# A hand-written order of 5341 pieces of work, replaced by another order of the same pieces

## The chip, the cores and the metric

The kernel runs on one core of a Trainium2 chip. The metric is device time in microseconds (us) of one execution. Before the change three runs gave 816.19, 816.78 and 819.2 us; their median is 816.78 us. A core has five engines, each of which works through its own list of instructions from the first to the last: TensorE (PE in the profile, with its weight loads as PEld), VectorE (DVE), ScalarE (ACT), GpSimd (POOL) and SyncE (SP, which here only issues transfers). They wait for each other through semaphores alone.

## The reference, cut to what matters

There are 8 batches of 8 heads with 576 positions and 64 features. First comes a thresholded attention per head, then a mixture of four causal attention experts over the 512 joined features of a batch, each position using the two experts with the largest gate:

```python
scores = scale * np.matmul(q, k.transpose(0, 1, 3, 2))
thresh = np.max(scores, axis=-1, keepdims=True) - tau
scores = np.where(scores >= thresh, scores, -1000000000.0)
attn = softmax(scores); x = np.matmul(attn, v)      # joined over heads: (B, S, 512)
for e in range(4):
    q, k, v = x @ wq[e], x @ wk[e], x @ wv[e]
    a = softmax(causal(scale * (q @ k.T)))
    out += (mask of the top 2) * gate weight * (a @ v @ wo[e])
```

## The kernel before, in words

Heads are taken in pairs: a pair fills the 128 partitions with 2 x 64 features. `n` counts the 32 pairs, four to a batch. For each pair the program has these pieces:

- `ldk`, `ldq`, `ldv`: transfers of keys, queries and values, issued by SP in its list's order (a few at the start by ACT).
- `tk`, `tq`: TensorE transposes keys and queries (line 1240). Then `kr`, `qr` copy them out of PSUM, `kh`, `qh` round them to the high part, and `kl`, `ql` subtract to get the low part (line 1087, in two halves). Products are made as high x high + high x low + low x high.
- `s`: scores, for five tiles of queries (numbered 4, 2, 3, 0, 1); tile 4 is the 64-position tails of both heads. It is the `kk,qq` matmuls of line 1103.
- `min` (line 1203, DVE): copies a score row block out of PSUM and finds its extremum. `exp` (line 1216, ACT). `thr`: a tiny sum. `stt` (line 1220, DVE): compares with the threshold, multiplies and sums. `eps1`, `rec1`: tiny. `pn` (lines 1498 and 1496): scales the rows, on POOL, ACT or DVE.
- `tm`: TensorE transposes the scaled rows (line 1240); `pt` copies them out (lines 1079, 1081, named `pa` and `pt`). `av`: the product with the values. `xr`, `xh`, `xl`, `xd` copy it out and split it into the high and low part of `x`.

After a batch's four pairs come its expert pieces: `pj` (projections, `x,wh` and `x,wl` matmuls), `v` (values and gates), `s2`, `s2t`, `nm`, `p2`, `p2s`, `t2`, `pt2`, `bv`, `zh`, `zl`, `o`, `ob`, `st`, alike in kind. The weights are loaded, rounded (`wh`) and subtracted (`wl`) once, during the first pairs; the first projection needs all of them and all of the first batch's `x`. Where a matmul group must cross the two halves of the array, a tiny fence instruction (`fs`, `fpj`, `fv`, `fo`, `fs2t`, lines 1357 and 1359) on another engine stands between its two parts.

What sets the order is a table written out by hand, `ORDER`: for each family of pieces one global place per piece, in 0 to 5340. `work()` makes the pieces, `plan()` goes through them by place and emits each on its engine, so that each engine's list is the sorted table cut down to that engine. A second table, `BY`, has for each piece that may run on several engines one digit, which of them it takes (0, 1 or 2 in the order in which the piece names its engines):

```python
x = Task({e: (u[0] - u[1], u[0]) for e, u in t.items()}, fn, deps, takes, uses, cols, ld, name, ORDER[family][i], by)
for t in sorted(tasks, key=lambda t: t.place):
```

`plan()` also picks the buffer slots and PSUM banks and puts a few small filler matmuls (`tri`) on TensorE at the start, from costs written in the file; these costs are the same before and after. The engines still wait on semaphores for real data, so a place in the tables decides what an engine waits for and never what is computed.

Of the kernel before, what the change touches and what calls it, by code (L numbers as in the profile page):

```python
# [248 lines left out]
def work(K):  # L249
# [320 lines left out]
    for n in range(NPR):  # L570
# [1019 lines left out]
```

## Time and profile before

| what | us |
|---|---|
| three runs | 816.19, 816.78, 819.2 |
| the profiled execution, its own time | 816.84 |
| its span from first to last instruction | 815.1 |
| TensorE busy | 791.2 |
| VectorE busy | 730.3 |
| ScalarE busy | 697.7 |
| GpSimd busy | 423.3 |

The profiled execution took 816.84 us, 0.06 us more than the median of the runs; 1.7 us of it lie around the span. An engine is busy while one of its instructions runs; waiting and issuing are not counted. A stretch's busy time is read from the view by windows, the wait in front of an instruction from the timeline, where it stands in square brackets with the engine that ended it.

### The profile page before, as it was taken

The numbers are of one execution on the slowest core, as the hardware profiler recorded it, in microseconds if no ns is written. First come the engines' busy times: TensorE is split into PE (matmuls) and PEld (weight loads), VectorE is DVE, ScalarE is ACT, GpSimd is POOL, SyncE is SP. The second block draws the span as 40 slices with busy tenths as digits, with TensorE's granted clock in tenths as the row PEclk, the third lists the DMA queues.
The fourth block names the chain that finished last, engine by engine and source line by source line (L and its number), as shares of the span: only waits on it lengthen the run. The fifth ranks groups of instructions, "written<-read, shape, count | busy, mean of one in ns | idle before, by whom it ended". The sixth has DMA issues, their size and how long they took to land.

```text
span 815.1 us, 34755 instructions
## 1 busy us (share of the span) xinstructions
PE 791.2 (97%) x14117; PEld 731.0 (90%) x14117; DVE 730.3 (90%) x2331; ACT 697.7 (86%) x1449; POOL 423.3 (52%) x811
## 2 busy tenths in 40 slices
PE   9888999999999999999999999999999999999998
PEld 7777898899988999888998999889998899988997
DVE  6999989998989989898989988998999988999584
ACT  5989888997899868998899988999999987999475
POOL 5998625753445345544365435455345563468232
PEclk9999999999999999999999999999999999999999
DMA  4433212112132112222222122202311212220002
GB/s 115 89 80 72 66 38 45 42 45 52 39 83 55 37 47 50 55 64 52 46 54 64 43 73 55 61 14 69 80 42 38 67 45 50 59 55 3 15 27 80
DMA packets 140240, 44.21 MB, mean 54 GB/s; under 512 B 135216, under 2 KB 135216, under 8 KB 140080
## 3 DMA queue, kind: packets, MB, share of 16 engines
q1 hardware_dynamic: 138512, 41.65, 20.9%
q8 instruction: 111, 1.82, 1.0%
q10 hardware_dynamic: 1568, 0.34, 0.2%
q14 instruction: 49, 0.40, 0.2%
HBM read 32.51 MB, written 9.44 MB: 51 GB/s over the span
## 4 chain that ended last, share of the span: by engine, by line
PE 76%; DVE 9%; ACT 6%; POOL 5%; issue 3%; DMA 1%; SPq 0%; DVEq 0%; ACTq 0%; POOLq 0%
PE ps L1103 64%; PE ps L1240 10%; DVE e L1203 3%; PE ps L1093 3%; POOL e L1498 2%; DVE e L1220 2%; ACT pt L1079 1%; ACT e L1216 1%; DMA ki<-in_k_dram 1%; ACT e L1475 1%; DVE e L1470 1%; POOL sm L1213 1%; ACT pa L1079 0%; DVE pt L1081 0%; ACT e L1490 0%
## 5 line engine op out<-in xcount | busy, mean ns | idle before, releaser
L1498 POOL TENSOR_SCALAR e<-e,sm 128x576 f32<-128x576 f32 (+4 forms) x277 | 193.5, 708 | 82.0 <-DVE sm L1231 55.3
L1203 DVE TENSOR_SCALAR_CACHE_REDUCE e<-ps 128x576 f32<-128x576 f32 x288 | 209.5, 752 | 21.2 <-PE ps L1103 15.5
L1216 ACT ACTIVATE e<-e,sm 128x576 f32<-128x576 f32 x288 | 215.3, 771 | 10.9 <-DVE e L1203 8.8
L1220 DVE SCALAR_TENSOR_TENSOR e<-e,sm,e 128x576 f32<-128x576 f32 x256 | 209.4, 841 | 2.4 <-ACT e L1216 0.7
L1103 PE MATMUL ps<-kk,qq 64*128 64x288 f32 x1900 | 176.1, 309 | 5.7 <-POOL kk L1087 1.3
L1103 PEld LDWEIGHTS ps<-kk,qq 64*128 64x128 f32 x1900 | 139.9, 186 | 16.1 <-DVE e L1203 3.4
L1079 ACT ACTIVATE pt<-ps 128x640 f32<-128x640 f32 (+3 forms) x228 | 142.5, 639 | 13.1 <-PE ps L1093 5.4
L1103 PE MATMUL ps<-pt,vm 128*64 128x128 f32 (+1 forms) x1536 | 143.9, 259 | 0.0
L1240 PE MATMUL ps<-ident,e 64*128 64x64 f32 x2624 | 123.8, 226 | 7.1 <-DVE e L1203 2.7
L1103 PEld LDWEIGHTS ps<-pt,vm 128*64 128x64 f32 x1536 | 127.3, 137 | 2.7 <-issue 0.7
L1240 PEld LDWEIGHTS ps<-ident,e 64*128 64x128 f32 x2624 | 108.8, 139 | 19.1 <-issue 5.1
L1103 PE MATMUL ps<-pa,vm 128*64 128x128 f32 x1024 | 124.4, 274 | 0.0
L1103 PEld LDWEIGHTS ps<-pa,vm 128*64 128x64 f32 x1024 | 110.7, 137 | 3.3 <-issue 1.2
L1103 PE MATMUL ps<-x,wh 64*128 64x288 f32 x1024 | 106.0, 296 | 0.0
L1213 POOL TENSOR_TENSOR sm<-sm 128x2 f32<-128x2 f32 (+1 forms) x127 | 41.9, 333 | 121.7 <-DVE e L1220 82.5
L1496 ACT ACTIVATE e<-e,sm 128x576 f32<-128x576 f32 (+4 forms) x116 | 83.2, 730 | 5.9 <-DVE sm L1231 4.8
L1103 PEld LDWEIGHTS ps<-x,wh 64*128 64x128 f32 x1024 | 84.2, 185 | 0.6 <-ACT kk L1142 0.2
L1103 PE MATMUL ps<-x,wl 64*128 64x288 f32 x512 | 78.5, 292 | 0.0
L1475 ACT ACTIVATE e<-e,sm 128x384 f32<-128x384 f32 (+3 forms) x128 | 70.9, 557 | 1.6 <-DVE sm L1470 1.0
L1079 ACT ACTIVATE pa<-ps 128x512 f32<-128x512 f32 x105 | 62.2, 595 | 7.0 <-PE ps L1240 6.8
L1470 DVE CUSTOM_DVE_ANT_0 e<-ps,tri 128x384 f32<-128x384 f32 (+3 forms) x128 | 58.4, 484 | 3.7 <-PE ps L1103 2.9
L1359 POOL TENSOR_SCALAR fencePOOL<-eps 128x2 f32<-128x2 f32 x56 | 16.7, 298 | 83.5 <-PE ps L1103 80.1
(153 smaller groups left out, 1656.5 us busy)
## 6 DMA issues: line engine op xcount, KB each, us to landing
vm<-in_v_dram SPq DMA_DIRECT2D x64, 128.0 KB, 2.6
out_dram<-ob SPq DMA_DIRECT2D x32, 256.0 KB, 2.4
ki<-in_k_dram SPq DMA_DIRECT2D x63, 80.0 KB, 2.5
qi<-in_q_dram SPq DMA_DIRECT2D x63, 80.0 KB, 2.5
ki<-in_k_dram SPq DMA_DIRECT2D x63, 64.0 KB, 2.4
vt<-in_v_dram SPq DMA_DIRECT2D x128, 16.0 KB, 2.2
qi<-in_q_dram SPq DMA_DIRECT2D x31, 64.0 KB, 2.4
qi<-in_q_dram SPq DMA_DIRECT2D x31, 48.0 KB, 2.4
```

The lines of the kernel that those rows point to most:

```text
L1079: self.nc.scalar.activation(dst, src, AF.Copy)
L1093: self.nc.tensor.transpose(self.ps[:, bank, c * n:(c + 1) * n], x[sl], self.ident[sl, sl])
L1103: return self.nc.tensor.matmul(out, x, y, start=first, stop=last)
L1203: self.nc.vector.tensor_scalar(self.sides(sc), self.dbank(s)[:, :, :HS], 0.0, None, op0=ALU.add, op1=ALU.min, accum_out=self.small(sm)[:, ...
L1213: self.nc.gpsimd.tensor_tensor(m[:, to:to + n], m[:, of:of + 2 * n:2], m[:, of + 1:of + 2 * n:2], op=ALU.add)
L1216: self.nc.scalar.activation(self.row(e), self.row(sc), AF.Exp, bias=self.small(sm)[:, 2 * j:2 * j + 1], scale=-1.0)
L1220: self.nc.vector.scalar_tensor_tensor(self.row(e), self.row(sc), m[:, 8 + j:9 + j], self.row(e), op0=ALU.is_le, op1=ALU.mult, accum_out=m[ ...
L1240: self.nc.tensor.transpose(self.ps[:, g.slot + h, c * D:(c + 1) * D], x, self.ident[sl, sl])
L1470: self.nc.vector.tensor_tensor_reduce(self.row(p2)[:, :w], self.dbank(g)[:, j, :w], self.tri[:, SM - w:], 1.0, FAR, op0=ALU.add, op1=ALU.m ...
L1475: self.nc.scalar.activation(p, p, AF.Exp, bias=m[:, 2 * j:2 * j + 1], scale=-1.0, accum_out=m[:, 4 + 2 * j:5 + 2 * j])
L1496: self.nc.scalar.activation(p, p, AF.Copy, scale=x)
L1498: (self.nc.vector if e == "DVE" else self.nc.gpsimd).tensor_scalar(p, p, x, 0.0, op0=ALU.mult, op1=ALU.add)
```

## The change

Only the numbers of the two tables change: nearly every place in `ORDER`, and many digits of `BY`. Two families of the second table show the kind of edit:

```diff
-    "xd": "00100011000100000000000000001111",
+    "xd": "00001000010000000100010000001011",
-    "kl": "000000010000000000000000000000000000",
+    "kl": "000000001000000000000000000000000000",
```

No piece is added or dropped. TensorE keeps the same 12140 instructions, the 89 filler matmuls among them, in a slightly different order. DVE goes from 1757 to 1738 instructions, ACT from 1313 to 1339, POOL from 816 to 809, SP stays at 599. Of the row scalings (lines 1498 and 1496), DVE had 39 and gets 15; ACT had 116 and gets 147; POOL had 277 and gets 270.

Two places show how the lists differ. The first is GpSimd's list where it prepares the keys of the fourth pair. `kk1_...` and `qq1_...` are that pair's keys and queries, `wh` and `wl` the weights' high and low part, `e` score rows, `x` and `iv` the first attention's output, `sm` small sums. Before:

```order
L1087 TENSOR_TENSOR kk1_61_918<-pt3_53_821,kk1_61_918 128x320
L1213 TENSOR_TENSOR sm_80<-sm_80 128x2
L1087 TENSOR_TENSOR qq1_63_936<-pt1_50_787,qq1_63_936 128x320
L1498 TENSOR_SCALAR e2_58_870<-e2_58_870,sm_80 128x576
L1087 TENSOR_TENSOR wl2_125<-ob0_54_823,wh2_122 128x256
L1083 TENSOR_SCALAR wh2_122<-sm_80 128x4
L1087 TENSOR_TENSOR wl2_125<-ob1_47_760,wh2_122 128x256
L1083 TENSOR_SCALAR x10_72_1030<-iv2_71_1026 128x256
L1087 TENSOR_TENSOR kk1_61_918<-pt3_53_821,kk1_61_918 128x320
```

And GpSimd's list at the same place with the change:

```order
L1498 TENSOR_SCALAR e7_45_730<-e7_45_730,sm_80 128x576
L1083 TENSOR_SCALAR qq1_60_922<-pt0_44_707 128x640
L1083 TENSOR_SCALAR x00_49_789<-iv1_46_742 128x256
L1083 TENSOR_SCALAR wh2_122<-ob2_28_505 128x256
L1083 TENSOR_SCALAR kk1_67_970<-pt3_56_858 128x640
L1087 TENSOR_TENSOR qq1_60_922<-pt0_44_707,qq1_60_922 128x320
L1087 TENSOR_TENSOR kk1_67_970<-pt3_56_858,kk1_67_970 128x320 x2
L1087 TENSOR_TENSOR qq1_60_922<-pt0_44_707,qq1_60_922 128x320
```

The second half of the keys' low part stood eight instructions behind the first, with two weight subtractions, a rounding of `x` and a row scaling between; now both halves follow each other.

The second place is VectorE's list just ahead of the first batch's first projection. `x20` and `x30` are the outputs of the third and fourth pair, `x00` and `x10` of the first and second. Before:

```order
L1087 TENSOR_TENSOR x20_109_1510<-iv4_95_1367,x20_109_1510 128x64
L1498 TENSOR_SCALAR e0_106_1500<-e0_106_1500,sm_80 128x576
L1220 SCALAR_TENSOR_TENSOR e5_111_1521,sm_80<-e4_104_1468,sm_80,e5_111_1521 128x576
L1203 TENSOR_SCALAR e1_117_1621,sm_80<-ps_63 128x576
L1203 TENSOR_SCALAR e2_118_1623,sm_80<-ps_63 128x576 x2
L1087 TENSOR_TENSOR x20_109_1510<-iv4_95_1367,x20_109_1510 128x320
L1087 TENSOR_TENSOR x00_46_758<-iv1_49_785,x00_46_758 128x256
L1220 SCALAR_TENSOR_TENSOR e5_111_1521,sm_80<-e4_104_1468,sm_80,e5_111_1521 128x576
L1074 TENSOR_REDUCE sm_80<-sm_80 128x2
L1231 RECIPROCAL sm_80<-sm_80 128x2
L1087 TENSOR_TENSOR x30_116_1619<-iv2_114_1592,x30_116_1619 128x320
```

And VectorE's list at the same place with the change, down to the last of the four `x` that the projection needs:

```order
L1203 TENSOR_SCALAR e3_116_1631,sm_80<-ps_63 128x576
L1203 TENSOR_SCALAR e0_118_1635,sm_80<-ps_63 128x576 x2
L1081 COPY pt1_122_1669<-ps_63 128x640
L1087 TENSOR_TENSOR wl1_124<-ob1_110_1527,wh1_121 128x256
L1087 TENSOR_TENSOR x30_120_1647<-iv0_115_1606,x30_120_1647 128x320
L1203 TENSOR_SCALAR e4_127_1738,sm_80<-ps_63 128x576
L1087 TENSOR_TENSOR x10_105_1464<-iv2_70_1027,x10_105_1464 128x320
L1087 TENSOR_TENSOR qq1_113_1590<-pt3_112_1580,qq1_113_1590 128x320
L1203 TENSOR_SCALAR e4_127_1738,sm_80<-ps_63 128x576
L1081 CAST x30_120_1647<-iv0_124_1731 128x256
L1087 TENSOR_TENSOR x30_120_1647<-iv0_124_1731,x30_120_1647 128x256
```

The row scaling and the subtractions for `x20` and `x00` have left VectorE's list (they run on other engines), and a weight subtraction, a copy out of PSUM and a rounding of `x30` have come to it. Counted from the start to the last of these subtractions, VectorE had 141 pieces of the table and now has 132; GpSimd, down to its own last piece that the projection needs, had 102 and now has 106.

## Rows read from the trace of the kernel before

**Rows 1.** Stretches: length, busy us (instructions) of PE, PEld, DVE, ACT, POOL, then PE's clock:

```profile
0.00:91.00 91.00, 79.53 (x1231) 67.85 (x1233) 81.19 (x228) 73.89 (x131) 76.08 (x127) 0.98 0.38 87
91.00:100.00 9.00, 9.00 (x150) 9.00 (x149) 8.98 (x26) 7.84 (x15) 3.01 (x6) 1.00 0.27 60
100.00:700.00 600.00, 592.65 (x10774) 552.15 (x10773) 553.11 (x1775) 531.37 (x1104) 291.42 (x572) 1.00 0.22 52
700.00:815.10 115.10, 110.07 (x1974) 101.96 (x1970) 87.01 (x306) 84.58 (x202) 52.82 (x109) 1.00 0.13 38
```

**Rows 2.** The same view of 20 to 91 us alone:

```profile
20.00:91.00 71.00, 61.34 (x1068) 53.56 (x1067) 67.92 (x187) 62.80 (x115) 65.84 (x92) 0.98 0.35 78
```

**Rows 3.** PE's waits, 0 to 91 us: who waited for whom, us, times, longest:

```profile
PE ps L1240 <- POOL e L1498: 2.5, 5, 0.8
PE ps L1103 <- DVE eps L983: 1.5, 1, 1.5
PE ps L1103 <- POOL kk L1087: 1.3, 1, 1.3
```

**Rows 4.** PE's waits from 91 us to the end, the longest total and the last:

```profile
PE ps L1103 <- ACT pt L1079: 1.4, 4, 0.5
...
PE ps L1240 <- ACT pt L1079: 0.2, 1, 0.2
```

**Rows 5.** Timeline of POOL: start us, us, instruction, [idle before]:

```profile
53.23 0.98 POOL L1087 TENSOR_TENSOR wl<-ob,wh 128x256 fp32r<-128x256 f32 x1
54.18 0.91 POOL L1083 TENSOR_SCALAR x<-iv 128x256 fp32r<-128x256 f32 x1
55.06 1.35 POOL L1087 TENSOR_TENSOR kk<-pt,kk 128x320 fp32r<-128x320 f32 x1
```

**Rows 6.** Timeline of PE at the matmuls that wait for these keys:

```profile
56.47 0.54 PE L1103 MATMUL ps<-kk,qq 64*128 64x288 f32 x4 [1.34 <-POOL kk L1087]
```

**Rows 7.** Timelines of DVE and PE where the first projection starts:

```profile
90.22 0.96 DVE L1087 TENSOR_TENSOR x<-iv,x 128x320 fp32r<-128x320 f32 x2
...
91.31 0.34 PE L1103 MATMUL ps<-x,wh 64*128 64x288 f32 x2
```

**Rows 8.** DVE's groups by shape, 0 to 91 us: count, busy us, mean ns:

```profile
L1220 DVE SCALAR_TENSOR_TENSOR e<-e,sm,e 128x576 f32<-128x576 f32 x34 | 33.3, 1001 | 0.0
L1498 DVE TENSOR_SCALAR e<-e,sm 128x576 f32<-128x576 f32 x2 | 1.5, 764 | 0.0
L1081 DVE CAST kk<-pt 128x640 fp32r<-128x640 f32 x1 | 1.1, 1082 | 0.0
L1087 DVE TENSOR_TENSOR x<-iv,x 128x256 fp32r<-128x256 f32 x2 | 0.8, 418 | 0.0
L1081 DVE COPY pt<-ps 128x640 f32<-128x640 f32 x1 | 0.8, 804 | 0.0
L1359 DVE TENSOR_SCALAR fenceDVE<-eps 128x2 f32<-128x2 f32 x1 | 0.5, 491 | 0.0
L1081 DVE CAST wh<-ob 128x256 fp32r<-128x256 f32 x1 | 0.5, 490 | 0.0
L1087 DVE TENSOR_TENSOR x<-iv,x 128x64 fp32r<-128x64 f32 x1 | 0.3, 345 | 0.0
```

**Rows 9.** POOL's groups in the same view and stretch:

```profile
L1498 POOL TENSOR_SCALAR e<-e,sm 128x576 f32<-128x576 f32 x22 | 20.5, 940 | 2.3 <-DVE sm L1231 2.3
L1087 POOL TENSOR_TENSOR kk<-pt,kk 128x320 fp32r<-128x320 f32 x7 | 7.1, 1012 | 1.4 <-ACT kk L1079 1.4
```

**Rows 10.** Groups by shape of 100 to 700 us:

```profile
L1220 DVE SCALAR_TENSOR_TENSOR e<-e,sm,e 128x576 f32<-128x576 f32 x198 | 156.7, 814 | 2.3 <-ACT e L1216 0.7
L1498 POOL TENSOR_SCALAR e<-e,sm 128x576 f32<-128x576 f32 x141 | 105.6, 756 | 64.3 <-DVE sm L1231 51.8 <-DVE sm L1074 5.2 <-PE ps L1103 3.4
L1496 ACT ACTIVATE e<-e,sm 128x576 f32<-128x576 f32 x74 | 55.7, 771 | 3.0 <-DVE sm L1231 2.8
```

**Rows 11.** Timeline of ACT at the end:

```profile
810.01 1.98 ACT L1079 ACTIVATE ob<-ps 128x512 f32<-128x512 f32 x3 [1.29 <-PE ps L1103]
```

More of the change, by code (lines that the diff above doesn't have):

```diff
@@ L588 @@
     "warm": [
-        12,
+        15,
     ],
     "tau": [
-        11, 18, 20,
+        12, 13, 28,
     ],
     "w": [
-        397, 498, 508, 259, 198, 278, 281, 25, 21, 29, 227, 142, 271, 354, 555, 22, 460, 495, 79, 233, 357, 406, 568, 358, 384, 362, 471, 302, 335, 484,
+        428, 502, 510, 91, 503, 506, 509, 25, 31, 33, 132, 142, 475, 508, 526, 18, 448, 476, 257, 360, 169, 195, 484, 292, 345, 540, 437, 318, 342, 554,
     ],
     "wh": [
-        552, 547, 299, 30, 61, 280, 180, 35, 502, 133, 319, 410, 447, 500,
+        525, 555, 125, 27, 44, 204, 295, 21, 496, 294, 388, 382, 552, 490,
@@ L774 @@
+        4981, 5093, 4989, 5073, 5084, 5092,
     ],
     "xd": [
-        529, 587, 525, 545, 1047, 1143, 1185, 1221, 1759, 1570, 1817, 1859, 2354, 2380, 2446, 2546, 2916, 3171, 2973, 3197, 3539, 3823, 3797, 3859, 4409, 4235, 4435, 4525, 5084,
-        5080, 5078, 5075,
+        505, 556, 469, 551, 741, 1214, 1183, 1241, 1731, 1798, 1882, 1843, 2431, 2524, 2428, 2543, 2932, 3045, 3106, 3202, 3491, 3840, 3848, 3861, 4175, 4351, 4448, 4522, 4786,
+        5042, 5025, 5086,
     ],
     "kr": [
-        81, 139, 258, 375, 559,
+        78, 164, 263, 363, 565,
@@ L781 @@
     ],
     "kl": [
-        104, 99, 195, 216, 301, 344, 413, 449, 592, 597, 619, 813, 979, 1134, 1304, 1463, 1690, 1841, 1953, 2139, 2332, 2506, 2591, 2722, 3030, 3164, 3239, 3406, 3664, 3818,
-        4004, 4067, 4238, 4440, 4664, 4745,
+        89, 103, 197, 202, 315, 311, 427, 446, 599, 623, 618, 821, 975, 1152, 1300, 1464, 1689, 1829, 1940, 2143, 2333, 2519, 2588, 2728, 3024, 3172, 3244, 3399, 3663, 3806,
+        3988, 4067, 4235, 4434, 4670, 4753,
     ],
     "qr": [
-        58, 132, 245, 372, 520,
+        55, 107, 216, 351, 523,
@@ L802 @@
+        2726, 2749, 2761, 3214, 3235, 3225, 3242, 3335, 3358, 3340, 3364, 3924, 3949, 3959, 3962, 3998, 4025, 4031, 4059, 4552, 4560, 4537, 4545, 4631, 4649, 4663, 4669, 5094,
+        5097, 5096, 5100, 5139, 5161, 5128, 5145,
     ],
     "fpj": [
-        610, 598, 676, 744, 1259, 1290, 1354, 1438, 1929, 1913, 2055, 1999, 2566, 2606, 2696, 2766, 3227, 3236, 3337, 3364, 3930, 3960, 4000, 4059, 4560, 4540, 4646, 4672, 5098,
-        5104, 5155, 5149,
+        612, 614, 666, 732, 1244, 1292, 1366, 1425, 1909, 1941, 2063, 2002, 2573, 2611, 2704, 2750, 3218, 3231, 3351, 3360, 3942, 3960, 4013, 4053, 4554, 4541, 4634, 4668, 5095,
@@ L818 @@
+        3891, 4577, 4596, 4605, 4612, 4583, 5107, 5111, 5108, 5114, 5112,
     ],
     "fv": [
-        654, 784, 1277, 1323, 1955, 1933, 2637, 2559, 3276, 3293, 3896, 3886, 4567, 4615, 5115, 5109,
+        645, 779, 1280, 1321, 1978, 1946, 2642, 2562, 3277, 3304, 3888, 3897, 4586, 4609, 5110, 5113,
     ],
     "v2": [
-        662, 801, 1298, 1356, 1983, 1950, 2652, 2575, 3282, 3317, 3923, 3910, 4598, 4626, 5123, 5124,
+        657, 801, 1298, 1352, 1988, 1966, 2648, 2586, 3296, 3312, 3914, 3906, 4598, 4620, 5117, 5120,
@@ L921 @@
+        5203, 5169, 5217, 5300, 5281, 5329, 5330, 5334,
     ],
     "ob": [
-        1137, 1144, 1217, 1244, 1722, 1874, 1827, 1804, 1902, 2370, 2798, 2491, 2461, 3102, 3165, 3124, 3109, 3174, 3645, 3792, 3768, 3843, 4433, 4408, 4471, 4466, 4520, 5096,
-        5228, 5187, 5234, 5315, 5306, 5331, 5339, 5335,
+        1141, 1146, 1239, 1227, 1727, 1869, 1818, 1802, 1902, 2376, 2805, 2488, 2463, 3091, 3149, 3124, 3100, 3178, 3646, 3784, 3779, 3847, 4423, 4404, 4465, 4469, 4534, 5118,
+        5229, 5183, 5235, 5309, 5306, 5339, 5332, 5336,
@@ L947 @@
-    "xd": "00100011000100000000000000001111",
+    "wh": "01111102110000",
+    "wl": "01000001000000",
+    "ldk": "000001000000000000000000000000000000000000000000000000000000000000000000000000000000000000000000000000000000000000000000000000000000000000000000000000000000000000000000000000000000000000000000",
+    "ldq": "1111000000000000000000000000000000000000000000000000000000000000000000000000000000000000000000000000000000000000000000000000000000000000000000000000000000000000",
+    "kh": "010101000000100000001100001010000",
@@ new lines @@
+    "qh": "00100100022001101000010120000210000001112000010100011001200012012",
+    "fs": "11211001110010010111000021120122",
+    "thr": "1212120222012222021020022210102001010221222110012011222120222001012101201020111002212001001211201102111210002220022100211212100000202200121110200220001120200220",
+    "eps1": "2210222001121020012000022120220120202120200020020002102221021202201122220220220022011002202201012210112100001202211122222100020121202222122100020100022221220020",
+    "pn": "200020020002220000100222000002020202222202020201202200002000000200000220220022220202210000002000002022202020202201202222000000000000002000020020020220020020202202000200200202200002220021202022220022002000020022000020212220020002220122002002000000002212220202220201222000002000000022000220",
@@ new lines @@
+    "pt": "000000001000000000000000000010000001000101000000000100010000100000011000010000000001001010000100010000011001100000100001000000001000000000000001001000000100001100010000000001000010000001000011000000011000000100000110000000100000000001000000000010111000101001000100001000010000010001001010",
+    "xr": "0000000000000000011100010000000000110010010100000010110000000000",
+    "xh": "0010001210000102010001010100010111001110000001121200101110101011",
+    "xl": "0010001110000011000000000000001000000100000100110000000000011111",
@@ L963 @@
-    "ob": "000001000000000100100000010000110000",
+    "ql": "0000000011000010010000000000000011000000000000100000000000000010000000110000000000000000000000001011",
+    "fpj": "11111122220102201221202222120221",
+    "qu": "01000010100100000000000010001000",
+    "qd": "01100000111111001200100202101110",
+    "fv": "0102111022021012",
+    "v2": "0000100000000000",
+    "shr": "11011110111111001111011101111101100111111100111000010001011100111000000101011101",
+    "p2s": "000000000000020222200000002020000220000200200000002020000000001000000000020020000000022000000000221020002202211000000020002211202000002000002020",
@@ L964 @@
+    "pt2": "0000011010000001000100010000000000010001000001010010000010100000000000000001000000010000000000001011001101010100",
+    "fs2t": "0112000122010202",
+    "zh": "111110000000111000000100001010000010000110110000",
+    "fo": "200001002200120210111201101220211022",
+    "ob": "000011010010000110000000100001011000",
 }
```

126 lines of the change are left out of this document (48 added, 78 removed), and 304 rows, old and new, of the table ORDER.

## The prediction

> **What bounds the kernel now.** I read the stretches first, then TensorE's waits on either side of 91 us, then timelines at the waits, then the groups by shape. The stretches [rows 1] show two different programs. From 100 us on TensorE is busy 592.65 of 600 us and 110.07 of 115.10 us; in the 9 us before that it never stops. Before 91 us it is busy 79.53 us of 91 and stands idle for 11.47. So of the 23.9 us in which TensorE does nothing, nearly half lie in the first ninth of the time. TensorE bounds everything behind 91 us, and something else bounds the start.
>
> What does so is seen in [rows 2]: between 20 and 91 us VectorE is busy 67.92 of 71 us (96%), GpSimd 65.84 (93%), ScalarE 62.80 (88%), TensorE 61.34 (86%). VectorE and GpSimd run full and TensorE waits for one or the other: 2.5 us in five waits for row scalings of GpSimd, 1.3 us in one wait for a key subtraction of GpSimd; 1.5 us is the first memory fill, which no order of the later pieces touches [rows 3]. The same two engines also get slower there. The `stt` of VectorE takes 1001 ns before 91 us [rows 8] and 814 ns later [rows 10]; the full-width scaling on GpSimd takes 940 ns [rows 9] and later 756 ns [rows 10]. The gate at the end of this stage is the first projection: it starts at 91.31 us, right behind VectorE's last two `x` subtractions, which run from 90.22 for 0.96 us, to 91.18 [rows 7].
>
> Behind 91 us the waits are short and many: the largest sum for one pair of engines is 1.4 us in four waits, and the list falls to single waits of 0.2 us [rows 4].
>
> **The change, part by part.** *TensorE's own work.* The same 12140 instructions, the 89 fillers included, in nearly the same order: cost 0 in itself. A matmul can only wait less or more. That caps the gain: 11.47 us before the gate less the 1.5 of the memory fill, so at most 10, and behind it 600 − 592.65 + 115.10 − 110.07 = 12.4 us, of which the end keeps its share (below).
>
> *The start, VectorE.* Down to the last `x` subtraction before the gate VectorE has 141 pieces and then 132; its 43 `min` and 38 `stt` stay. It loses, from [rows 8], one rounding of keys (1.08 us), one row scaling (0.76), one fence (0.49), one weight rounding (0.49), one small (0.35) and two larger `x` subtractions (2 x 0.42), which is 4.0 us; it gains one copy out of PSUM (0.80). One half of a keys' subtraction goes and one of queries comes, which cancel; two tiny sums and one `x` rounding go as well and are not counted. Sum: −3.2 us on an engine that is 96% busy and releases the gate.
>
> *The start, GpSimd.* 102 pieces become 106. It takes one scaling more (0.94) and two `x` subtractions, which I price at the 1.01 us of the keys' subtraction [rows 9]; a half of keys' subtraction comes and one of queries goes; a rounding, a small subtraction and a sum come, a rounding and a fence go, about nothing. Sum: +2.9 us. It has 71 − 65.84 = 5.2 us free between 20 and 91 us [rows 2], so this fits in, but without much to spare.
>
> *The start, single waits.* The keys of the fourth pair show what the order buys. GpSimd runs a weight subtraction (0.98), an `x` rounding (0.91) and then the second half of the keys' low part, until 56.41 [rows 5]; TensorE's score matmuls wait 1.34 us for it [rows 6]. In the new list both halves follow each other, ahead of the weights, and this wait has nothing to stand on. What comes late instead are the weight pieces, which nobody needs before the gate.
>
> So the gate moves by somewhere between −3.2 us (VectorE alone decides) and 0 (GpSimd's 2.9 more fill its 5.2 free us in the wrong places and its pieces come just as late as before). I take −2.5: VectorE's chain is what ended last at the gate, and the one wait of 1.34 us is surely gone.
>
> One rule speaks against part of it. What the two engines do to each other here is seen in [rows 8, 10]: `stt` is 1001/814 = 1.23 times as long where GpSimd is busy 93% of the time. The Trainium skill (GPSIMD Engine Reference, 1. Specifications) says that GpSimd shares its SBUF interfaces with VectorE and contends with VectorE instructions that have two SBUF inputs, which `stt` has; the trace agrees. By that rule the 2.9 us more on GpSimd would slow the `stt` beside them: these take 33.3 of 91 us, so 2.9 x 0.37 x 0.23 = 0.25 us, and the sum would be −2.25.
>
> *Behind the gate.* ScalarE takes over full-width scalings: 24 more at 771 ns [rows 10] is 18.5 us over the whole kernel, less some copies that go to VectorE. Pro rata 18.5 x 600/815 = 13.6 us fall between 100 and 700 us, where ScalarE would go from 531.37 to at most 545 of 600 us (91%), just under VectorE, which stands at 553.11 (92%) and is relieved of scalings. These scalings lie beside TensorE, which is the bound there; I cost them at 0. Should the cover go, each one that stands in front of a copy TensorE needs costs up to its 0.77 us. The single waits behind the gate will fall elsewhere; bounds −3 and +3 us on what they add up to, about a half of the 7.35 us of idle time in 100 to 700 us either way, and 0 as the value.
>
> *The end.* The last three copies out run from 810.01 for 1.98 us [rows 11], and the transfer behind them ends the span at 815.1. The last steps of the new order are again a projection's second part, a copy on ScalarE and a store: 0.
>
> Sum: −2.5 + 0 + 0 against the profiled 816.84 us, which gives 814.3. That execution is 0.06 us from the runs' median of 816.78, so the same number stands for the median.
>
> **The rivals.** *The start gets much better.* If VectorE's load falls by 3.2 us and the pieces are also laid so that the two engines hinder each other half as much, 34 `stt` win 0.094 us each, 3.2 us more: −6.4, 810.4 us. For it: that is where the slow pieces are. Against it: with GpSimd at 93%, and more to do, there is little room to keep them apart. I give it 0.24.
>
> *The order is another, the time is not.* GpSimd takes over the gate: its 2.9 us more come to lie before its last `x` piece, which eats VectorE's gain, and the short waits of the rest only change places: 816.8 us. For it: 5.2 us of free time and an engine that TensorE already waits for most. 0.17.
>
> *ScalarE comes late.* Behind the gate ScalarE, at up to 91%, holds both the copies out of PSUM and the new scalings in one list. TensorE's longest total there is already for such a copy (1.4 us, [rows 4]). If a third of the 24 scalings stand ahead of a copy that is just due, TensorE waits 8 x 0.77 = 6.2 us: 816.84 + 6.2 = 823.0 with no gain at the start. It decides from five or six such places on (4.1 us). Against it: the copy can be placed first, and VectorE is relieved by the same step. 0.17.
>
> **How the numbers follow.** About 0.5%, or 4.1 us, is what a measurement of this kernel can tell from no change: faster is below 812.7, slower above 820.9. My forecast, 814.3, has 0.42; with the bounds of its terms, −3.2 to 0 at the start and −3 to +3 behind it, it reaches from 810.6 to 819.8, and a fifth of it (0.08) falls below 812.7. Faster is then 0.24 + 0.08 = 0.32, slower 0.17, and the rest, 0.34 + 0.17 = 0.51, is no change. The range for 8 in 10 leaves out the best part of the first rival and most of the last: 809.5 to 821.
>
> **What would show it.** In the changed profile the first projection (`x,wh`) should start near 88.8 us, not 91.3; TensorE's idle time before it should be near 9 us, and the wait for `kk` of GpSimd should be gone. Behind it TensorE should be idle about as long as now, 12 us. If the projection starts at 91 or later with GpSimd's piece last in front of it, the second rival holds. If TensorE's waits for ScalarE's `pt` behind 91 us, now 1.4 us [rows 4], grow to 5 or more, the third does. I am wrong outright if the start changes by less than 1 us and the time still moves by more than 4: then the short waits behind 91 us, which I count as 0, decide.

## The result: slower by 0.6%

With the change the kernel takes 821.63 us (median of 7 runs, 820.63 to 825.07), against 817.47 us of the kernel before in the same series; the ratio is 1.0063, with a 95% interval of 1.0048 to 1.0078. It is slower by 4.2 us by the medians and by some 5 us by the ratio, where 2.5 us less had been forecast. TensorE's clock is not the reason: single executions with a mean granted clock of 1.000 took 820.63 and 821.56 us with the change, and 815.67 and 815.92 us before. The profiled execution took 822.15 us, its span 820.4 us.

The stretches of the changed kernel, in the columns of [rows 1]:

```profile
0.00:91.00 91.00, 79.47 (x1223) 66.73 (x1223) 80.88 (x216) 74.92 (x136) 79.37 (x131) 0.98 0.40 89
91.00:100.00 9.00, 8.04 (x126) 7.80 (x128) 8.86 (x24) 6.66 (x12) 3.25 (x9) 1.00 0.08 18
100.00:700.00 600.00, 590.46 (x10736) 549.08 (x10734) 548.57 (x1756) 531.91 (x1116) 286.33 (x562) 1.00 0.22 52
700.00:820.40 120.40, 114.24 (x2040) 106.26 (x2038) 89.41 (x319) 91.78 (x214) 48.88 (x104) 0.99 0.13 39
```

Length less TensorE's busy time gives its idle time. To 91 us it is 11.53 us, where it was 11.47 [rows 1]; from 91 to 100 us 0.96, where it was 0; from 100 us on 9.54 + 6.16 = 15.7, where it was 7.35 + 5.03 = 12.4. So 4.3 of the 5.3 us are idle time, one part of it up to 100 us and three behind. The other 1.0 us is TensorE busy for longer (792.2 us, before 791.2). Counted by matmuls, 2.2 us are lost near 134 us: the 2000th starts at 136.1 us, before 133.9.

Now the start alone, with the last 16 us before the gate and three stretches of 2 us for the clock. First the changed kernel, then the kernel before:

```profile
20.00:91.00 71.00, 61.44 (x1070) 53.03 (x1066) 68.98 (x181) 62.92 (x114) 69.12 (x97) 0.98 0.37 82
75.00:91.00 16.00, 13.09 (x226) 11.41 (x222) 15.00 (x34) 11.74 (x22) 15.83 (x27) 0.89 0.28 62
84.00:86.00 2.00, 1.75 (x33) 1.75 (x35) 1.18 (x3) 1.71 (x5) 2.00 (x5) 0.77 0.19 43
86.00:88.00 2.00, 2.00 (x19) 1.72 (x17) 1.95 (x2) 2.00 (x5) 2.00 (x4) 0.50 0.59 134
88.00:90.00 2.00, 2.00 (x36) 1.70 (x32) 2.00 (x5) 0.69 (x2) 1.92 (x4) 0.88 0.46 106
```

```profile
75.00:91.00 16.00, 12.84 (x244) 11.22 (x242) 15.79 (x43) 12.99 (x24) 13.63 (x21) 1.00 0.24 53
```

The line to see is the second: GpSimd is busy 15.83 of 16 us (before 13.63), ScalarE only 11.74 (before 12.99). Between 20 and 91 us VectorE did not get emptier: 68.98 us, before 67.92 [rows 2]. TensorE's waits to 91 us, in the columns of [rows 3]:

```profile
PE ps L1240 <- POOL e L1498: 3.6, 6, 0.9
PE ps L1240 <- ACT iv L1079: 1.7, 1, 1.7
```

The wait for the keys (1.3 us, [rows 3, 6]), which stood behind two weight pieces in GpSimd's list [rows 5], is gone, as predicted. In its place stands a new one of 1.67 us, whose chain the timelines of GpSimd, ScalarE and TensorE show:

```profile
79.01 1.36 POOL L1087 TENSOR_TENSOR wl<-ob,wh 128x256 fp32r<-128x256 f32 x1
80.34 1.38 POOL L1087 TENSOR_TENSOR x<-iv,x 128x320 fp32r<-128x320 f32 x1
...
82.30 0.32 POOL L1087 TENSOR_TENSOR x<-iv,x 128x64 fp32r<-128x64 f32 x1
...
82.64 0.44 ACT L1079 ACTIVATE iv<-ps 128x320 f32<-128x320 f32 x1 [2.10 <-POOL x L1087]
...
83.14 0.53 PE L1240 MATMUL ps<-ident,e 64*128 64x64 f32 x10 [1.67 <-ACT iv L1079]
```

GpSimd still holds the first pair's output (`iv`) for two late subtractions; ScalarE needs that buffer to empty a PSUM bank for the fourth pair; TensorE waits for the bank. The first projection then starts at 92.42 us, before 91.31 [rows 7], while VectorE's last `x` subtraction is still running:

```profile
92.42 0.43 PE L1103 MATMUL ps<-x,wh 64*128 64x288 f32 x4
...
92.30 0.98 DVE L1087 TENSOR_TENSOR x<-iv,x 128x256 fp32r<-128x256 f32 x1
```

VectorE's groups by shape down to that point, of the changed kernel and then of the kernel before (whose other groups are in [rows 8]):

```profile
L1220 DVE SCALAR_TENSOR_TENSOR e<-e,sm,e 128x576 f32<-128x576 f32 x34 | 32.8, 993 | 0.1
...
L1087 DVE TENSOR_TENSOR qq<-pt,qq 128x320 fp32r<-128x320 f32 x2 | 1.9, 966 | 0.0
L1087 DVE TENSOR_TENSOR wl<-ob,wh 128x256 fp32r<-128x256 f32 x1 | 1.8, 1774 | 0.2 <-ACT wh L1079 0.2
...
L1087 DVE TENSOR_TENSOR x<-iv,x 128x320 fp32r<-128x320 f32 x2 | 1.5, 754 | 0.0
```

```profile
L1087 DVE TENSOR_TENSOR x<-iv,x 128x320 fp32r<-128x320 f32 x3 | 1.6, 520 | 0.0
...
L1087 DVE TENSOR_TENSOR qq<-pt,qq 128x320 fp32r<-128x320 f32 x1 | 0.5, 480 | 0.0
...
L1087 DVE TENSOR_TENSOR wl<-ob,wh 128x256 fp32r<-128x256 f32 x1 | 0.4, 445 | 0.0
```

The `stt` take what they took (993 against 1001 ns), but these subtractions of VectorE are 1.5 to 4 times as long. Where, the timelines of VectorE and GpSimd in the changed kernel show:

```profile
86.05 1.77 DVE L1087 TENSOR_TENSOR wl<-ob,wh 128x256 fp32r<-128x256 f32 x1 [0.16 <-ACT wh L1079]
87.74 1.03 DVE L1087 TENSOR_TENSOR x<-iv,x 128x320 fp32r<-128x320 f32 x1
...
89.37 0.48 DVE L1087 TENSOR_TENSOR x<-iv,x 128x320 fp32r<-128x320 f32 x1
89.77 1.02 DVE L1087 TENSOR_TENSOR qq<-pt,qq 128x320 fp32r<-128x320 f32 x1
...
86.08 0.73 POOL L1087 TENSOR_TENSOR x<-iv,x 128x256 fp32r<-128x256 f32 x1
86.78 0.73 POOL L1087 TENSOR_TENSOR wl<-ob,wh 128x256 fp32r<-128x256 f32 x1
87.49 0.94 POOL L1498 TENSOR_SCALAR e<-e,sm 128x576 f32<-128x576 f32 x1
...
89.40 1.05 POOL L1087 TENSOR_TENSOR wl<-ob,wh 128x256 fp32r<-128x256 f32 x1
```

The `x` at 89.37 us, which began just ahead of GpSimd's piece, took 0.48 us; the other three ended about 0.3 us behind a piece of GpSimd. On GpSimd, in the columns of [rows 9], the keys' subtractions got shorter (1012 to 870 ns) and the scalings did not:

```profile
L1498 POOL TENSOR_SCALAR e<-e,sm 128x576 f32<-128x576 f32 x23 | 21.9, 957 | 0.3 <-DVE sm L1231 0.3
...
L1087 POOL TENSOR_TENSOR kk<-pt,kk 128x320 fp32r<-128x320 f32 x8 | 6.8, 870 | 0.1
```

Between 100 and 700 us single pieces cost what they did: the `stt` 813 ns (814 in [rows 10]) and GpSimd's scaling 755 (756). What differs there is mainly waits, of which the longest of the kernel before was 0.5 us [rows 4]. From 91 us to the end, now:

```profile
PE ps L1103 <- DVE e L1203: 2.0, 5, 0.7
PE ps L1093 <- POOL e L1498: 1.4, 3, 0.9
PE ps L1103 <- ACT pt L1079: 1.3, 4, 0.5
PE ps L1240 <- ACT pt L1079: 1.3, 3, 0.5
PE ps L1240 <- DVE zt L1087: 0.8, 1, 0.8
```

Three single waits of 0.8 to 0.9 us stand near 248, 545 and 811 us. The timelines of TensorE and ScalarE show the second, and TensorE's the third:

```profile
545.93 0.59 PE L1093 MATMUL ps<-ident,e 64*128 64x64 f32 x12 [0.91 <-POOL e L1498]
547.06 0.46 PE L1240 MATMUL ps<-ident,e 64*128 64x64 f32 x8 [0.54 <-ACT pt L1079]
...
544.36 0.22 ACT L1079 ACTIVATE zt<-ps 128x64 fp32r<-128x64 f32 x1 [1.02 <-DVE z L1087]
...
812.05 0.38 PE L1103 MATMUL ps<-woh,z 64*128 64x256 f32 x1 [0.87 <-DVE z L1087]
```

At the end the first output tile is given the pair of PSUM banks that the last subtraction still reads; before, it had a free pair.

### The profile page after: what moved, and what is told of

Its sections match the earlier page's. It is cut to its first block, busy times and chain, and to the rows that moved or that the text cites. A ratio compares the mean times of both kernels' runs of the same rounds, so it can differ in the third digit from the quotient of the medians.

```text
span 820.4 us, 34790 instructions
## 1 busy us (share of the span) xinstructions
PE 792.2 (97%) x14117; PEld 729.9 (89%) x14117; DVE 727.7 (89%) x2312; ACT 705.3 (86%) x1475; POOL 417.8 (51%) x804
## 4 chain that ended last, share of the span: by engine, by line
PE 45%; ACT 4%; DVE 4%; issue 1%; POOL 1%; POOLq 0%; ACTq 0%; DVEq 0%
PE ps L1103 38%; PE ps L1240 6%; PE ps L1093 1%; ACT e L1475 1%; DVE e L1203 1%; ACT pt L1079 1%; ACT e L1216 1%; DVE e L1220 1%; DVE pt L1081 0%; ACT pa L1079 0%; DVE e L1470 0%; POOL e L1498 0%; ACT e L1496 0%; DVE fenceDVE L1359 0%; ACT e L1490 0%
## 5 line engine op out<-in xcount | busy, mean ns | idle before, releaser
L1498 POOL TENSOR_SCALAR e<-e,sm 128x576 f32<-128x576 f32 (+4 forms) x270 | 188.4, 706 | 92.2 <-DVE sm L1231 56.7
L1103 PE MATMUL ps<-kk,qq 64*128 64x288 f32 x1900 | 174.6, 307 | 3.7 <-DVE e L1203 1.8
L1079 ACT ACTIVATE pt<-ps 128x640 f32<-128x640 f32 (+3 forms) x226 | 140.3, 637 | 12.5 <-PE ps L1093 7.2
L1103 PEld LDWEIGHTS ps<-kk,qq 64*128 64x128 f32 x1900 | 139.5, 186 | 13.0 <-DVE e L1203 3.3
L1103 PE MATMUL ps<-pt,vm 128*64 128x128 f32 (+1 forms) x1536 | 144.4, 259 | 0.3 <-DVE e L1203 0.2
L1240 PE MATMUL ps<-ident,e 64*128 64x64 f32 x2624 | 120.6, 226 | 12.7 <-POOL e L1498 4.0
L1103 PEld LDWEIGHTS ps<-pt,vm 128*64 128x64 f32 x1536 | 128.0, 137 | 3.2 <-DVE e L1203 0.8
L1240 PEld LDWEIGHTS ps<-ident,e 64*128 64x128 f32 x2624 | 104.5, 138 | 27.3 <-POOL e L1498 10.0
L1103 PE MATMUL ps<-pa,vm 128*64 128x128 f32 x1024 | 125.0, 275 | 0.0
L1103 PEld LDWEIGHTS ps<-pa,vm 128*64 128x64 f32 x1024 | 111.4, 138 | 3.4 <-issue 1.3
L1496 ACT ACTIVATE e<-e,sm 128x576 f32<-128x576 f32 (+4 forms) x147 | 103.0, 720 | 6.6 <-DVE sm L1231 6.2
L1103 PE MATMUL ps<-x,wh 64*128 64x288 f32 x1024 | 106.1, 295 | 0.4 <-DVE e L1203 0.4
L1103 PEld LDWEIGHTS ps<-x,wh 64*128 64x128 f32 x1024 | 85.1, 185 | 1.6 <-DVE e L1203 0.8
L1103 PE MATMUL ps<-x,wl 64*128 64x288 f32 x512 | 79.3, 292 | 0.0
L1079 ACT ACTIVATE pa<-ps 128x512 f32<-128x512 f32 x101 | 58.9, 593 | 6.7 <-PE ps L1240 6.4
L1103 PE MATMUL ps<-wh,x 64*128 64x260 f32 x576 | 60.0, 284 | 0.2
```

The lines of the kernel that those rows point to most:

```text
L1079: self.nc.scalar.activation(dst, src, AF.Copy)
L1103: return self.nc.tensor.matmul(out, x, y, start=first, stop=last)
L1240: self.nc.tensor.transpose(self.ps[:, g.slot + h, c * D:(c + 1) * D], x, self.ident[sl, sl])
L1496: self.nc.scalar.activation(p, p, AF.Copy, scale=x)
L1498: (self.nc.vector if e == "DVE" else self.nc.gpsimd).tensor_scalar(p, p, x, 0.0, op0=ALU.mult, op1=ALU.add)
```

## The experiments

Each kernel was timed in five rounds beside the kernel before, and its ratio to that kernel is given with the 95% interval; the changed kernel's is 1.0063 (1.0048 to 1.0078). Line numbers in rows of x1 to x4, x6 and x7 are 4 lower than in the kernel, in the others 155 higher (L1258 is L1103): there a table holds each piece in the buffer slot that it had, so that a moved piece does not move slots elsewhere.

### Which part of the order

x1 and x2 cut both lists at one piece near 120 us and join the halves:

```diff
 x1:  places and engines up to s2t.0.04  - before  + changed
 x2:  places and engines from s2t.0.04   - before  + changed
 x10: x1, fence of s2t.0.04  - GpSimd, behind two pieces of q  + VectorE
```

**x1.** 

> The changed order (and its engines) up to the first transposition of an expert's scores, s2t.0.04, near 120 us; the order of before from there on. Theory: the change loses in two places, about 2.2 us up to 134 us (the 2000th matmul starts at 136.1 instead of 133.9 us) and about 3 us in single waits behind it. Then this kernel keeps the first loss alone: 817.5 + 2.2 = 819.7 us. Rival 1 (the start alone is to blame, and what follows is only carried along): 821.6. Rival 2 (the start costs nothing, the rest does): 817.5.

**x2.** 

> The other half: the order of before up to the same piece, the changed order from there on. Theory: 817.5 + 3 = 820.5 us, with the waits of 0.77 us (near 248 us), 0.91 us (near 545 us) and 0.87 us (near 811 us) in the trace again. Rival 1 (start alone): 817.5. Rival 2 (rest alone): 821.6.

**x10.** 

> As x1 (the changed order to near 120 us, the order of before behind it), slots held as in x1, without the wait of 1.43 us that the joint of the two orders made at 122 us: the fence of s2t.0.04 stands on VectorE instead of behind GpSimd's pieces. Theory (the two starts are equal; the first projection began at 91.9 us in x1 and at 92.3 in x2, whose start is that of before): 818 us, no difference from before that can be measured. Rival (the changed start costs 2 us of its own): 819.6 us.

Measured: x1 821.03 us, 1.0041 (1.0027 to 1.0054); x2 821.35 us, 1.0043 (1.0027 to 1.0059); x10 821.25 us, 1.0036 (1.0023 to 1.0049). Neither half alone is to blame, and neither is free: the new start costs some 3 us, the new rest some 3.5 us, which together is a little more than the whole and within the intervals. x10 refutes my theory that the starts are equal. First projections that lie within about 1 us of each other in single traces do not decide it: the kernel before has 91.31 us, x1 91.92, the changed kernel 92.42, and x2, whose start is that of before, 92.27, in an execution in which TensorE waited 2.13 us for a load of keys and the granted clock fell twice, from 24 to 34 us and from 72 to 78 us.

### Places or engines

```diff
 x6:  ORDER  - before  + changed      BY  before
 x7:  ORDER  before                   BY  - before  + changed
```

**x6.** 

> The changed table of places with the old table of engines (809 of its 2379 digits differ). If the places carry the loss, 821.6 us or more; if the pieces that changed engine carry it, about 817.5. The two tables may also only fit each other: then both this and x7 are slower than the changed kernel, at 823 or more.

**x7.** 

> The old table of places with the changed table of engines. If the engines carry the loss, 821.6 us or more; if the places carry it, about 817.5; if the tables only fit each other, 823 or more, as x6.

Measured: x6 926.24 us, 1.1322 (1.1296 to 1.1348); x7 933.73 us, 1.1424 (1.1395 to 1.1453). The third case holds, and by a factor of twenty more than I had written: 110 us. The tables only fit each other. My reading, which no run takes further: a piece sent to another engine at an unchanged place stands in a list that has no room for it. TensorE's waits spread over all engines; the longest sum of x6 and then of x7:

```profile
PE ps L1099 <- ACT fenceACT L1353: 8.8, 10, 2.0
```

```profile
PE ps L1236 <- POOL e L1494: 9.5, 10, 3.5
```

### Taking single waits of the start away

```diff
 x3, GpSimd:  + xl.0.2 xd.0.2   xh.1.0 xl.2.2 w wh   + pn.3.1   wl   - xl.0.2   w   - xd.0.2 ... - pn.3.1
 x5:  x3, GpSimd:  + pn.4.3   wl xl.1.0 xl.2.0 wl   - pn.4.3
      wh, wh, wh, xh.2.0   - GpSimd  + ScalarE
 x11, GpSimd of the kernel before:  + kl.3   wl w wl xh.1.0   - kl.3
```

**x3.** 

> The changed kernel, with two subtractions of the first pair's x (xl.0.2, xd.0.2) put four places earlier in GpSimd's list, ahead of weight pieces, and one row scaling (pn.3.1) ahead of a weight subtraction. Nothing changes engine. They free the buffer iv for which ScalarE waits 2.10 us at 82.6 us. Theory: TensorE's waits of 1.67 us (at 81.5 us) and 0.59 us (at 83.7 us) go, and the granted clock no longer falls to 0.50 at 86 to 88 us; the first projection starts 2 to 3 us earlier, at 89.5 to 90.5 us instead of 92.4, and the time is 821.6 - 2.5 = 819.1 us. Rival (GpSimd is full in the start, so what is put forward sends as much back): the projection stays within 0.5 us of 92.4, time 821.6.

**x5.** 

> As x3, with the buffers' slots held as in the changed kernel, one more scaling (pn.4.3, for which TensorE waited 1.92 us in x3) put ahead of a weight subtraction on GpSimd, and four roundings (three of weights, one of x; 2.2 us on GpSimd in the changed kernel) given from GpSimd to ScalarE. Theory now (GpSimd's whole list down to the first projection sets the gate, it is busy 69.1 of 71 us): the first projection starts at 89.5 to 90.5 us, against 92.4 in the changed kernel and 91.6 in x3, and the time is 819.5 us. Rival (VectorE, busy 69.0 of the same 71 us, sets it as well): the projection stays at 91.3 or later and the time at 821.5.

**x11.** 

> The kernel before, slots held, with one piece moved: the second half of the fourth pair's key subtraction (kl.3) four places earlier on GpSimd, ahead of two weight subtractions and a rounding. It takes away the one wait of 1.34 us that the prediction took as surely won. By the prediction's step the first projection starts 1.3 us earlier, near 90.0 us, and if the granted clock no longer falls behind that wait another 1.7 us earlier: 816.2 to 814.5 us. Theory now (the start is full on VectorE and GpSimd, a wait of TensorE taken away there comes back before the gate): projection at 91 to 92 us, 817.5 us.

Measured: x3 821.89 us, 1.0044 (1.0030 to 1.0058), not separable from the changed kernel. The wait of 1.67 us is gone and that of 0.59 us behind it is now 0.72, but 5 us later TensorE waits 1.92 us for the next scaling of GpSimd, and the clock falls there instead. TensorE's timeline and the windows of x3:

```profile
89.09 0.53 PE L1236 MATMUL ps<-ident,e 64*128 64x64 f32 x10 [1.92 <-POOL e L1494]
```

```profile
90.00:92.00 2.00, 1.50 (x22) 1.26 (x20) 1.97 (x4) 1.69 (x3) 2.00 (x6) 0.78 0.42 92
92.00:94.00 2.00, 2.00 (x20) 2.00 (x20) 1.90 (x8) 1.74 (x3) 1.26 (x3) 0.50 0.22 49
```

x5: 825.49 us, 1.0095 (1.0074 to 1.0116), slower, and by my own edit: one of the weight roundings given to ScalarE waits for a scaling of that weight late in GpSimd's list, and the copy that TensorE needs stands behind it. ScalarE and TensorE of x5:

```profile
83.54 0.42 ACT L1234 ACTIVATE wh<-ob 128x256 fp32r<-128x256 f32 x1 [2.89 <-POOL ob L1467]
...
85.36 0.90 PE L1395 MATMUL ps<-ident,e 64*128 64x64 f32 x12 [3.20 <-ACT iv L1234]
```

So x5 tells nothing of its question. x11: 818.01 us, 1.0000 (0.9989 to 1.0010). The 1.34 us that the prediction called surely won are worth nothing: the wait is gone from the trace, others take its place, and the projection starts at 92.49 us (in that execution a load of keys also came 2.4 us late). The theory holds by the time; what took the wait's place in the other executions no trace shows.

### Taking waits behind the start away

```diff
 x4:  x3, VectorE near 247 us:  + zl.1.04   nm.1.14 zl.1.03 zl.1.02   - zl.1.04
      GpSimd near 543 us:  + p2s.4.02   pn.22.3 pn.22.3 xh.21.0 thr.22.0   - p2s.4.02
      end:  PSUM pair of o.7.2  - 6  + 4
 x8:  x5, the last two edits of x4 and zh.4.04 (ScalarE)  + ahead of zh.4.14  - behind zl.4.03
 x9:  x2, the edits of x4 and x8 and exp.22.0 (ScalarE)  - ahead of pt2.4.12  + behind it
```

**x4.** 

> As x3, and three single waits behind the start mended as well: zl.1.04 ahead of nm.1.14 on VectorE (the wait of 0.77 us near 248 us), p2s.4.02 ahead of two row scalings on GpSimd (0.91 and 0.54 us near 545 us), and at the end the output of tile 2 takes a free pair of PSUM banks instead of the one that the last subtraction zl.7.12 still reads (0.87 us near 811 us). Theory (few long waits make the loss): x3 less 2.5 to 3 us, 816 to 816.6 us, under the kernel before. Rival (the waits are the sum of many small shifts; a mended one is replaced by the next): within 1 us of x3.

**x8.** 

> As x5, and behind the start: zh.4.04 ahead of zh.4.14 in the order, so that ScalarE no longer waits 1.02 us for VectorE in front of it (544.36 us), p2s.4.02 ahead of two row scalings on GpSimd, and at the end the output of tile 2 takes a free pair of PSUM banks. Theory (a wait goes only when every link of its chain is moved): the waits of 0.91 and 0.54 us near 545 us go and the end wins 0.6 us, so x5 less 2 us, 817.5. Rival (waits move on to the next piece): within 0.7 us of x5.

**x9.** 

> As x2 (the order of before to near 120 us, the changed order behind it), slots held as in x2, with three places mended: zl.1.04 ahead of nm.1.14 on VectorE (0.28 us of the wait near 248 us in x4); near 545 us zh.4.04 ahead of zh.4.14, p2s.4.02 ahead of two scalings and exp.22.0 behind the copy pt2.4.12 (0.91 and 0.54 us); at the end a free pair of PSUM banks for tile 2 (0.87 us). Theory (these few waits are most of what the changed order loses behind the start): x2's 821.35 less 2.6 = 818.8 us. Rival (many small shifts): 820.6 us or more.

Measured: x4 821.58 us, 1.0043 (1.0031 to 1.0055), the same as x3; the rival holds. In its trace only the wait at the end is gone. That near 248 us shrank to 0.48, those near 545 us stayed at 0.90 and 0.54, now put down to ScalarE's copy: a second link of the same chain that had been just as late. Moving the small copy `zh.4.04`, for which ScalarE stood 1.02 us, turned 0.91 into 0.32 in x8 and x9. x8: 823.47 us, 1.0073 (1.0054 to 1.0092), 2.0 us under x5 as expected, with intervals that overlap. x9: 819.81 us, 1.0028 (1.0016 to 1.0040), 1.5 us under x2 by the medians and 1.2 by the ratios, where 2.6 had been expected and 0.7 by the rival: it lies between. These few waits are part of what the rest loses, not most of it.

### The same work on ScalarE

```diff
 x12, kernel before:  kh.4 xh.2.2 xh.2.0   - VectorE  + ScalarE
 x13, kernel before:  kh.4 xh.2.2 xh.2.0   - VectorE  + GpSimd
 x15:  x12 and  wh xh.1.0   - GpSimd  + ScalarE
 x14, changed kernel:  wh xh.1.0 xh.2.0   - GpSimd  + ScalarE;  qh.5   - VectorE  + ScalarE
 x16:  x14 and the edits of x9 behind the start
```

**x12.** 

> The kernel before, slots held, with three roundings of the start (kh.4, xh.2.2, xh.2.0, 2.6 us on VectorE) given from VectorE to ScalarE and nothing to GpSimd. By the prediction's premise (VectorE's chain sets the gate) the first projection starts 2 to 2.6 us earlier, near 89 us, and the time is 815.2 us. Rival (GpSimd sets it, or ScalarE's list comes late with the added pieces): projection at 91 us or later, 817.5 us or more.

**x13.** 

> The kernel before, slots held, with the same three roundings as x12 (kh.4, xh.2.2, xh.2.0) taken from VectorE, but given to GpSimd instead of ScalarE. Theory (GpSimd is as full as VectorE in the start, so what it takes over comes back at the gate): projection at 91 to 93 us and 817.5 to 819.5 us. Rival (it is enough to relieve VectorE, as the prediction had it, GpSimd having 5.2 us free): near x12, projection at 89 us and 815.5 us.

**x15.** 

> As x12, with two more roundings of the start (a weight rounding of 0.99 us and xh.1.0 of 0.91 us) given from GpSimd to ScalarE. xh.1.0 stands in front of the key subtraction for which TensorE waits 1.33 us at 55 us. Theory: that wait falls to about 0.4 us and another 1 us is won at the gate: 814.3 us. Rival (ScalarE is now the full one, busy 15.66 of the last 16 us before the gate in x12): no gain over x12's 815.4, or a loss of up to 2 us.

**x14.** 

> The changed kernel, slots held, order untouched, with four roundings of the start given to ScalarE: wh, xh.1.0 and xh.2.0 from GpSimd (1.8 us) and qh.5 from VectorE (1.1 us). They fill the 2.10 us in which ScalarE waits at 80.5 us. Theory (the changed start is late because GpSimd got the work and ScalarE idles): TensorE's wait of 1.67 us at 81.5 us shrinks to about 0.3, the projection starts near 90.3 us instead of 92.4, time 821.6 - 2.1 = 819.5 us. Rival (the order itself is at fault): projection at 92 us or later, 821.5 us.

**x16.** 

> x14 with the waits near 248, 545 and 811 us mended as in x9. Theory (start and those places are the loss): x14 less 1.2 us (what x9 won over x2), 818.3 us, within 0.2% of before. Rival (the loss lies in many small shifts): as x14, or over 820 us.

Measured: x12 815.37 us, 0.9963 (0.9951 to 0.9975), faster than both kernels; x13 817.03 us, 0.9981 (0.9971 to 0.9991); x15 815.32 us, 0.9966 (0.9954 to 0.9979). Three roundings less on VectorE are worth 3.0 us by the ratios if ScalarE takes them and 1.6 us if GpSimd does: relieving VectorE wins with either receiver, so it is one of the engines that set the gate, and GpSimd seems to give about half of the gain back (the two intervals just overlap). Part of x12's lead is TensorE's clock: among executions with a mean granted clock of 0.995 to 0.997, x12 (4 of them) is 2.4 us ahead of the kernel before by the medians and x13 (5) is 0.8 us ahead. Windows and first projection of x12:

```profile
20.00:91.00 71.00, 62.44 (x1114) 54.70 (x1113) 68.92 (x194) 66.96 (x124) 68.70 (x94) 1.00 0.37 82
75.00:91.00 16.00, 15.05 (x274) 13.44 (x273) 15.90 (x46) 15.66 (x31) 13.99 (x20) 1.00 0.28 63
...
88.29 0.43 PE L1258 MATMUL ps<-x,wh 64*128 64x288 f32 x4
```

In x12 TensorE is busy 15.05 of the last 16 us before 91 us (12.84 before), and ScalarE 15.66 (12.99 before). The projection of x13 began at 91.89 us, but its trace held a late load of keys (1.2 us) and two falls of the clock, where that of x12 held none, so the times, not these two starts, are the comparison. x15 wins nothing over x12: the wait for the keys is gone from its trace, and the time is the same. ScalarE was as full there (15.67 of the last 16 us) as in x12, which is the rival's reason; no run tests it alone.

x14: 822.25 us, 1.0045 (1.0031 to 1.0059), not separable from the changed kernel, where 819.5 us had been expected; its profiled execution took 829.04 us (the other five 820.86 to 822.56) and held a wait of 4.9 us, so its start is not compared. Ahead of that wait VectorE ran one `stt`, from 48.63 us, for 5.89 us (0.81 us is usual), while GpSimd ran eight pieces one behind the other, down to 53.92 us; the `stt` ended 0.6 us behind the last of them. x16: 820.64 us, 1.0035 (1.0022 to 1.0048): both mends together win 0.28 of the 0.63%. In its trace the start is as good as before: the projection begins at 91.30 us, and the 1500th matmul some 0.1 us earlier than in the kernel before. By the 14000th it is 3.35 us later. GpSimd is as full as in the changed kernel (15.92 of the last 16 us before 91 us), so that alone does not fix the gate. About 3 us of loss behind the start remain after all named waits have been mended.

## Why the prediction was wrong, step by step

*TensorE's own work, 0.* Nearly right: 4.3 of 5.3 us are idle time.

*The start, VectorE, −3.2 us: the step that failed first.* The nine pieces did leave, but their time did not: down to its last `x` subtraction VectorE was busy 81.37 us before and 83.12 us now. Two things were wrong. The first is the list. VectorE gave two copies of queries to ScalarE and got two roundings of queries; the counts cancel and the sum left them out, but the copies lay at 6.9 and 7.5 us, behind a wait of 5.2 us, and the roundings lie at 60.2 and 80.9 us, where VectorE is full. VectorE's group before, then with the change:

```profile
L1081 DVE COPY qq<-ps 128x320 f32<-128x320 f32 x2 | 1.0, 488 | 5.2 <-PE ps L1240 5.2
...
L1081 DVE CAST qq<-pt 128x640 fp32r<-128x640 f32 x2 | 2.1, 1050 | 0.0
```

That is 2.1 us more in the full stretch; with it, and with the `x` rounding (0.71 us) and the tiny sums that were not counted, the term was worth 1 to 2 us and not 3.2. The second is the price. I priced what left and took what stayed at its old duration. Beside a GpSimd that is busy 99% of the last 16 us it grew: `wl` 1774 − 445 = 1.33 us, two `qq` at 966 − 480 = 0.97, two `x` of 320 columns at 754 − 520 = 0.47, the last `x` of 256 columns 980 − 418 = 0.56 [rows 8], the row scaling 1116 − 764 = 0.35. That is 3.7 us, more than the 3.2. The `stt`, on which alone I had put 0.25 us of contention, did not change. The Trainium skill (GPSIMD Engine Reference, 1. Specifications) names VectorE instructions with two SBUF inputs as those that contend with GpSimd; these subtractions have two, and the traces agree in part. In the changed kernel four of 910 to 1027 ns began with 0.56 to 0.70 us of a GpSimd piece still to run and ended 0.28 to 0.35 us behind it; the `wl` of 1774 ns began in the last 0.08 us of a small piece and ended 0.31 us behind the second of the two larger ones that followed. In the kernel before, `qq` at 53.1 us and `kk` at 71.6 us took 480 and 481 ns although a two-input piece of GpSimd began within 0.1 us behind them, and so did an `x` in the changed kernel at 89.37 us (481 ns, GpSimd's `wl` beginning 0.03 us later). So the order of beginning seems to matter, though it does not explain the `wl`; this is read from two traces, and no run was made to test it. That relieving VectorE does move the gate, and that the place where the work went was wrong, x12 shows: with ScalarE as the receiver the time falls by 3.0 us. That its projection began at 88.29 us, where I had put it (88.8), is in part luck: the clock did not fall in that start, and its fall in the kernel before was worth 1.7 us.

*The start, GpSimd, +2.9 us in 5.2 free us.* The size was right (65.84 to 69.12, +3.3 us), the room was not: free time counted over 71 us is no room in the last 16, where GpSimd went from 13.63 to 15.83. This is near the second rival, which I had priced at no loss, though its sign (GpSimd's piece last in front of the gate) did not come: VectorE's `x` was last. The new start as a whole costs about 3 us (x10); of that, GpSimd's share is shown only by x13 against x12, where the same work costs some 1.4 us more on GpSimd than on ScalarE, with intervals that just overlap.

*The start, single waits, 1.34 us surely won.* The wait went and nothing came of it (x11: ratio 1.0000). I take it that in a stretch where two engines are full, a wait of TensorE shows where the lack of room comes out, not what makes it; x3, where a mended wait was followed by another, agrees.

*Behind the gate, 0 with bounds of ±3.* This term failed as well. Idle time there grew by 3.3 us, just beyond the bound. x2 measures the loss of this part as 0.27 to 0.59%, 2.2 to 4.8 us. What I had written would prove me wrong outright (the start moves by less than 1 us, the time by more than 4) came nearly true: 1.1 and 5.3.

*ScalarE comes late, the third rival.* Not as I had put it: TensorE's waits for `pt` at the two lines shown went from 1.4 + 0.2 [rows 4] to 1.3 + 1.3 us, not to 5, and ScalarE's busy time between 100 and 700 us rose by 0.5 us, not by up to 13.6. It came up in x5, by my own edit.

*The end, 0.* The projection there waits 0.87 us for a PSUM pair; behind it nothing changed: from ScalarE's last copies to the end it is 820.4 − 815.23 = 5.2 us, before 815.1 − 810.01 = 5.1 [rows 11].

What stays open: of the loss behind the start, x9 and x16 take back about 1 to 1.5 us at three places. The remaining 2.3 to 3.4 us are not settled, and their cause stays open. In x16 TensorE's idle time behind the start is 2.4 us more than in the kernel before (10.89 against 8.52 us, counted from the 1500th matmul), in waits of which only one exceeds 0.5 us (0.54), and about 1 us is TensorE busy for longer, which no experiment here explains.

## What to carry to other kernels

Price a move by the engine that receives the work and by its load in the last stretch before the gate, and reprice what stays on the neighbours beside it. Compare kinds and not only counts when a list of pieces changes. Before believing that a wait is won, ask whether an engine of that stretch has free time; if it has none, look for one that has and move work there: with ScalarE in the kernel before (12.99 of 16 us) that won 3.0 us (x12); with ScalarE in the changed kernel (11.74 of 16 us) it won nothing that can be told from the noise (x14). An order and its choice of engines belong together: changing either alone cost 13 to 14% here.

## What the runs showed of the hardware

- TensorE's granted clock fell behind stalls of the start, but not behind every one. In the changed kernel, after 80 to 84 us, in which TensorE was busy 1.47 and 0.53 of 2 us, it was 0.77, 0.50 and 0.88 in the next three stretches, the lower of its two levels (1.2 GHz) for some 3.4 us, worth 1.7 us (2 x 0.23 + 2 x 0.50 + 2 x 0.12). In x3 the stall moved to 87 us and the fall with it, to 90 us and later. In the kernel before it fell behind the wait for the keys (and one of 0.67 us for a load), as the two windows below show, and was worth 1.7 us too: between these two traces the fall makes no difference. No fall followed in x10, whose waits of 1.66 and 0.59 us are those of the changed kernel (busy 0.38 of 2 us from 82 to 84 us, clock 1.00) and whose projection still began at 92.50 us; in x12, with the same wait for the keys (1.33 us); or in the kernel before, where a pair of stretches was busy 1.40 and 0.92 of 2 us (82 to 86 us). These traces do not tell which stalls cost a fall.

```profile
58.00:60.00 2.00, 1.96 (x21) 1.99 (x23) 0.88 (x5) 1.13 (x3) 2.00 (x3) 0.55 0.55 121
60.00:62.00 2.00, 1.93 (x28) 1.79 (x26) 1.31 (x6) 0.79 (x2) 1.82 (x4) 0.60 0.39 88
```

- Where VectorE's two-input subtractions ran long beside GpSimd, VectorE paid: at 86 us its `wl` took 1.77 us while two such pieces of GpSimd beside it took 0.73 each. In the profiled execution of x14 an `stt`, which has two inputs as well, took 5.89 us beside a GpSimd that never paused (its median in that trace is 0.81 us).
- In traces whose order is that of before at that place, TensorE's wait for a load of keys near 26 us was anything from none (the kernel before, x12) to 2.42 us (x11). x2's projection, behind a wait of 2.13 us, began 0.96 us later than that of the kernel before: a single trace of this start does not decide about 1 us.
